# Last two token groups of an MLP as block products of Strassen's form, and state products in 64-column pieces

## The chip, the core and the metric

The kernel runs on one core of a Trainium2 chip. The metric is the device time of one execution in microseconds. The core has TensorE (PE, matrix products; weight loads are listed as PEld), VectorE (DVE), ScalarE (ACT), GpSimd (POOL) and SyncE (SP, which issues all the DMAs here). Each engine takes its instructions in the order in which they stand in its own queue.

## The reference

A gated linear recurrence over 768 tokens for 4 batches and 8 heads of 48 x 48 complex states, and then an MLP with a leaky activation on the 3072 tokens:

```python
a_re_n, a_im_n = a_re * scale, a_im * scale      # scale = min(|a|, 0.999) / (|a| + 1e-6)
for t in range(S):
    S_re, S_im = ar * S_re - ai * S_im + kv, ar * S_im + ai * S_re   # kv = k[t] outer v[t]
    y[:, :, t] = einsum('bhd,bhde->bhe', q[:, :, t], S_re)
x = y.transpose(0, 2, 1, 3).reshape(3072, 384)
h = x @ w_in                                     # 384 -> 2048
out = (max(h, 0) + alpha * min(h, 0)) @ w_out    # 2048 -> 384
```

All products are in float32. `w_in` and `w_out` come as float64 and are converted on the chip.

## The kernel before

The recurrence is cut into 24 *units* of 128 tokens (4 batches of 6). `gates` (nine stretches of tokens) makes the products of decays and phases on DVE, ACT and POOL and leaves them in DRAM; `loads` and `loads_v` bring a unit's operands back. `unit(u)` turns q and k by the phases (L663, L665), scales them in steps of doubling distance (`step`, L718), and after each pair of steps multiplies keys with queries into `ps_lv` (L680). Then it transposes the keys (`ps_kt`, L789) into the tile `T`, makes two state products per unit from `T` and `V` (`ps_kv`, L799: 64 tokens of contraction, 96 weight columns and 48 moving columns for each head and half; the last unit of a batch makes only one), applies the level products (`ps_y`, L819) and the states (`ps_y`, L843), copies the result into `T` (L857) and sends it to DRAM (`ysc`).

The MLP follows in groups of tokens: groups 0, 1 and the last two hold one unit, the ten between hold two. `loads_x` loads a group's `ysc` as `xT` (three blocks of 128 input features). `features(m, f)` makes one of the 16 blocks of 128 hidden features in three products (`ps_h`, L891), each over all tokens of the group (256 or 128 columns); ACT takes the negative part (L898) and DVE adds the leaky term into the ring `g_sb` (L900). `outputs(m, c, f)` adds one feature block to the 128 x 384 result of one unit (`ps_o`, L910); after 16 blocks ACT copies it out (L920) and SP stores it (L923).

PSUM has eight banks: `ps_lv` 2, `misc` (`ps_kt`, `ps_kv`) 1, `ps_y` 2, `ps_h` 2, `ps_o` 1. All of this is written as generators that yield once per step. `Plan.run` walks the string `ORDER`: each letter continues one generator by one step, and so the string alone sets the order in every engine's queue, the DMAs on SP included. The arguments of a yield (`PE(0.72, ...)`, `takes=`) have no effect when the kernel is built: `step` returns None. What an instruction waits for comes from the tiles that it reads and writes.

## Time and profile before

| what | value |
|---|---|
| time, median of 3 runs | 838.25 us (837.62 to 840.72) |
| profiled execution: time, span from first to last instruction | 837.42 us, 835.7 us |
| granted TensorE clock, mean | 0.992 |
| PE busy in 0:100, 300:400, 500:600, 600:700 us | 12.4, 98.2, 99.3, 100.0 us |
| DVE busy in the same stretches | 82.4, 91.2, 83.3, 61.4 us |
| `ps_h` products L891, busy | 297.4 us |
| `ps_o` products L910, busy | 295.0 us |
| `ps_kv` products L799, busy | 38.9 us |
| POOL busy after 700 us | 0 us |

The span is what the rows of the profile add up to; the time of a run also has what lies around the span. A product of float32 shows as two instructions, so 704 instructions of L799 are 352 products. "Idle before" names what ended the wait of an engine ahead of a group of instructions. A row's duration is from an instruction's start to its end; on PE consecutive ones overlap, so what one costs is read from start to start.

### The profile page before, as it was taken

How to read it: one execution, taken by the hardware profiler on the slowest of the kernel's cores; microseconds unless marked ns; L12 is line 12 of the kernel's file. 1: busy time of each engine (PE TensorE's matmuls, PEld its weight loads, DVE VectorE, ACT ScalarE, POOL GpSimd, SP SyncE). 2: the span in 40 equal slices, each digit the busy share in tenths (PEclk: the TensorE clock that was granted, in tenths of full speed). 3: DMA queues.
4: the chain of work that ended last, by engine and by line, in shares of the span. 5: the costliest groups of instructions: out<-in, count | busy, mean ns of one | idle time of the engine just before them, and what ended most of it. 6: DMA issues, size and time to landing. Idle time of an engine off the chain costs nothing.

```text
span 835.7 us, 25314 instructions
## 1 busy us (share of the span) xinstructions
PE 701.3 (84%) x10784; PEld 533.9 (64%) x10784; DVE 637.5 (76%) x905; ACT 432.4 (52%) x893; POOL 282.6 (34%) x352
## 2 busy tenths in 40 slices
PE   0001317589999999999999999999999999999998
PEld 0001316467777777777777777776777777777776
DVE  5988979999999998989978989896649555542112
ACT  7787678377556644863675366624333333323221
POOL 5379399357306620661453127303220000000000
PEclk9999999699999999999999999999999999999999
DMA  7584975885688479538863966457446635401110
GB/s 221 169 239 133 307 226 135 234 222 147 176 234 199 114 217 250 140 84 245 227 158 83 275 176 162 145 158 186 100 98 176 159 95 125 103 24 36 42 29 10
DMA packets 186984, 130.82 MB, mean 157 GB/s; under 512 B 74744, under 2 KB 177272, under 8 KB 186488
## 3 DMA queue, kind: packets, MB, share of 16 engines
q1 hardware_dynamic: 186872, 129.20, 57.6%
q8 instruction: 85, 1.39, 0.7%
q14 instruction: 27, 0.22, 0.1%
HBM read 100.82 MB, written 35.71 MB: 163 GB/s over the span
## 4 chain that ended last, share of the span: by engine, by line
PE 63%; DVE 12%; POOL 7%; DMA 7%; ACT 6%; issue 3%; SPq 2%; DVEq 0%; ACTq 0%; POOLq 0%
PE ps_o L910 25%; PE ps_h L891 24%; PE ps_lv L680 4%; POOL gate L341 3%; PE ps_kv L799 3%; PE ps_y L819 3%; DMA T<-decs 2%; DVE KQ L718 2%; PE ps_y L843 2%; POOL run L343 2%; DVE gate L341 2%; DMA PP<-phs 1%; DMA phs<-gate 1%; DVE gate L429 1%; PE ps_kt L789 1%
## 5 line engine op out<-in xcount | busy, mean ns | idle before, releaser
L891 PE MATMUL ps_h<-xT,w_in_sb 128*128 128x256 f32 (+1 forms) x1344 | 297.4, 355 | 13.7 <-DMA xT<-ysc 13.5
L910 PE MATMUL ps_o<-w_out_sb,g_sb 128*128 128x384 f32 x768 | 295.0, 499 | 3.3 <-DVE g_sb L900 2.7
L891 PEld LDWEIGHTS ps_h<-xT,w_in_sb 128*128 128x128 f32 x1344 | 234.8, 193 | 85.5 <-DMA xT<-ysc 12.9
L898 ACT ACTIVATE g_sb<-ps_h 128x256 f32<-128x256 f32 (+1 forms) x224 | 79.0, 353 | 214.4 <-PE ps_h L891 213.3
L900 DVE SCALAR_TENSOR_TENSOR g_sb<-g_sb,al,ps_h 128x256 f32<-128x256 f32 (+1 forms) x224 | 97.9, 437 | 118.9 <-ACT g_sb L898 118.3
L910 PEld LDWEIGHTS ps_o<-w_out_sb,g_sb 128*128 128x128 f32 x768 | 136.0, 191 | 56.2 <-DVE g_sb L900 4.6
L718 DVE TENSOR_TENSOR KQ<-KQ,T 96x1024 f32<-96x1024 f32 x120 | 147.8, 1232 | 27.0 <-PE ps_lv L680 16.4
L341 POOL TENSOR_TENSOR gate<-gate 128x72 f32<-128x72 f32 (+1 forms) x56 | 42.5, 759 | 177.2 <-ACT gate L371 170.9
L680 PE MATMUL ps_lv<-WQ 96*32 96x32 f32 x2304 | 34.5, 202 | 76.4 <-DVE WQ L663 53.7
L680 PEld LDWEIGHTS ps_lv<-WQ 96*32 96x32 f32 x2304 | 26.2, 115 | 98.1 <-DVE WQ L663 53.7
L741 ACT COPY WQ<-KQ 96x1024 f32<-96x1024 f32 x48 | 50.0, 1041 | 23.7 <-DVE KQ L718 23.6
L341 DVE TENSOR_TENSOR gate<-gate 128x576 f32<-128x576 f32 (+3 forms) x70 | 46.8, 669 | 1.0
L341 POOL TENSOR_TENSOR gate<-run,runs 128x12 f32<-128x12 f32 x46 | 36.8, 800 | 31.2 <-ACT runs L371 28.1
L757 ACT COPY W<-KQ 96x512 f32<-96x512 f32 x48 | 30.8, 642 | 27.3 <-DVE KQ L718 23.2
L429 DVE TENSOR_TENSOR gate<-gate 128x1152 f32<-128x1152 f32 (+2 forms) x36 | 44.5, 1257 | 0.1
L518 POOL TENSOR_SCALAR top<-top 128x768 f32<-128x768 f32 x16 | 39.7, 2486 | 14.3 <-ACT top L510 14.2
L694 ACT ACTIVATE A<-ps_lv,columns 128x64 f32<-128x64 f32 x144 | 37.6, 335 | 8.4 <-PE ps_lv L680 8.3
L799 PEld LDWEIGHTS ps_kv<-V,T 64*96 64x96 f32 x704 | 35.9, 167 | 9.1 <-issue 4.6
L857 ACT COPY T<-ps_y 48x256 f32<-48x256 f32 x96 | 32.0, 365 | 18.2 <-PE ps_y L843 17.4
L321 POOL TENSOR_TENSOR gate<-gate 128x72 f32<-128x72 f32 (+5 forms) x24 | 22.5, 939 | 54.8 <-DVE gate L321 53.8
L799 PE MATMUL ps_kv<-V,T 64*96 64x48 f32 x704 | 38.9, 252 | 2.1 <-ACT T L791 2.0
L819 PE MATMUL ps_y<-A,VL 64*48 64x64 f32 x2304 | 38.8, 221 | 0.3 <-issue 0.3
(104 smaller groups left out, 943.7 us busy)
## 6 DMA issues: line engine op xcount, KB each, us to landing
T<-decs SPq DMA_DIRECT2D x48, 384.0 KB
PP<-phs SPq DMA_DIRECT2D x24, 387.0 KB
KQ<-in_q_dram SPq DMA_DIRECT2D x48, 192.0 KB
decs<-gate SPq DMA_DIRECT2D x7, 1152.0 KB
phs<-gate SPq DMA_DIRECT2D x14, 576.0 KB
KQ<-in_k_dram SPq DMA_DIRECT2D x40, 192.0 KB
vsc<-in_v_dram SPq DMA_DIRECT2D x48, 144.0 KB
VL<-vsc SPq DMA_DIRECT2D x48, 144.0 KB
```

Source lines behind the costliest of these rows:

```text
L341: on(4 * k).tensor_tensor(out=m, in0=w[:, 1::-1].unsqueeze(2).to_broadcast([P, 2, 2, k]), in1=pairs_of(u), op=ALU.mult)
L429: TT(out=m[:, a], in0=U5[:, 1 + a], in1=turned(off3, o)[:, a].unsqueeze(1).unsqueeze(3).to_broadcast([P, L // 2, nb, 2]), op=ALU.mult)
L518: nc.gpsimd.tensor_scalar(out=top, in0=top, scalar1=F64_SMALL, scalar2=None, op0=ALU.max)
L680: nc.tensor.matmul(t[64 * i + j:64 * i + j + HC // 2, p], lhsT=keys(n, g), rhs=queries(n, g), start=True, stop=True)
L718: nc.vector.tensor_tensor(out=x, in0=x if x0 is None else x0, in1=m, op=ALU.mult)
L741: nc.scalar.copy(z.rearrange("p i n t -> p i (n t)").rearrange("p i (m h) -> p m i h", h=h), bass.AP(tensor=KQ.tensor, offset=KQ.offset + ...
L799: nc.tensor.matmul(kv[s][:, n], lhsT=T[rows, n, 0:D2], rhs=V[rows, n // 2, (n % 2) * D:(n % 2 + 1) * D], start=True, stop=True)
L819: nc.tensor.matmul(o, lhsT=Vp[h][64 * i:64 * i + 64, s, e_ * D:(e_ + 1) * D], rhs=a, start=False, stop=False)
L891: nc.tensor.matmul(p, lhsT=w_in_sb[:, f // 2, kk, f % 2 * P:(f % 2 + 1) * P], rhs=x_of[m][:, kk], start=(kk == 0), stop=(kk == NK - 1))
L898: nc.scalar.activation(gt, p, AF.Relu, scale=-1.0)
L900: nc.vector.scalar_tensor_tensor(out=gt, in0=gt, scalar=al_1[:, f:f + 1], in1=p, op0=ALU.mult, op1=ALU.add)
L910: nc.tensor.matmul(sums[0], lhsT=gt[:, c * P:(c + 1) * P], rhs=w_out_sb[:, f], start=(f == 0), stop=(f == NF - 1))
```

## The change

Groups are now 1, 1 and eleven of two units; the last two groups (units 20, 21 and 22, 23) go through `late_features` and `late_outputs`.

- `late_features(m, j)` makes two feature blocks for 256 tokens at once. The first two blocks of input features, the two units and the two feature blocks form a product of 2 x 2 by 2 x 2 blocks of 128, made with seven products (Strassen, in Winograd's form) in place of eight; the third input block is added by two products of 256 columns. They need differences of `x` (`tx`, four DVE subtractions per group) and of `w_in` (`mixes`, DVE, in a freed gate buffer). Seven partial sums lie in two PSUM banks, alternately `ps_y` and the two of `ps_h`; five DVE additions and one ACT copy join them in `g_sb`, then ACT and DVE apply the activation.
- `late_outputs` does the same for the second part: two units, two feature blocks, two halves of 192 output features. The sums of activations are made on POOL (four additions of 128 x 128 per pair of blocks, in KQ buffers), those of `w_out` in `mixes`. Seven products of 192 columns per pair add up over eight pairs in seven half banks of `ps_lv`, `misc` and `ps_o` (here `ps_m`); at the end one ACT copy and seven DVE operations make the 256 x 384 result, which goes out in two stores.
- In `unit`, a state product has its 96 weight columns extended to 128 (32 columns of the transposed keys are copied twice) and is made in two pieces of 64 columns.
- `ysc` has eight DRAM buffers in place of four, and `ORDER` is another string.

```diff
-    "AAMMBBAJAJAAMMMAJAAAAAAAAAAABAAAAAAAAAKABAKBAAAAAKABJOAKBAMAABAABAAOABLAKAOOAAKAANAABBKAABALABBABBAN"
...
+    "AABBMMAAAAAAAAAAABMMMKAAJAAABKABJAJAAKAAAAABAJBAAAANAMAKBAAKABAKANAANNBABBBABBKBBMABAKAOABLKABBALNOA"
...
+    "qqqqqqqqqqqqqqqqq")
...
-    sizes = [1, 1] + [MC] * ((NU - 4) // MC) + [1, 1]
+    sizes = [1, 1] + [MC] * ((NU - 2) // MC)
+    LATE = len(sizes) - 2
...
-            e = yield ACT(HP * D2, e, ("decays", u))
+            e = yield ACT(HP * P + 80, e, ("decays", u))
             nc.scalar.copy(T[:, 4 * i:4 * (i + 1), 0:D2], t)
+            nc.scalar.copy(T[:, 4 * i:4 * (i + 1), D2:P], t[:, :, 0:P - D2])
             R["misc"].put(e)
-        e = yield PE(0.72, e, ("V", u), *[("state", u - 1)] * (u > 0), takes=(R["misc"],) if last else (R["misc"], R["lv"]), mode=2, n=8 if last else 16)
+        e = yield PE(0.72, e, ("V", u), *[("state", u - 1)] * (u > 0), takes=(R["misc"],) if last else (R["misc"], R["lv"]), mode=2, n=16 if last else 32)
         V = L["V"]
-        kv = [ps.tile([P, H, D], F32, tag=tag, name="ps_kv", bufs=n)[0:D2] for tag, n in (("misc", 1), ("lv", 2))[:2 - last]]
+        kv = [ps.tile([P, H, D], F32, tag=tag, name="ps_kv", bufs=n) for tag, n in (("misc", 1), ("lv", 2))[:2 - last]]
         for n in range(H):
-            for s in range(1 if last else 2):
-                rows = slice(HC * s, HC * (s + 1))
-                nc.tensor.matmul(kv[s][:, n], lhsT=T[rows, n, 0:D2],
-                                 rhs=V[rows, n // 2, (n % 2) * D:(n % 2 + 1) * D], start=True, stop=True)
+            for j in range(0, P, HC):
+                for s in range(1 if last else 2):
+                    rows = slice(HC * s, HC * (s + 1))
+                    nc.tensor.matmul(kv[s][j:j + HC, n], lhsT=T[rows, n, j:j + HC],
+                                     rhs=V[rows, n // 2, (n % 2) * D:(n % 2 + 1) * D], start=True, stop=True)
...
-            nc.vector.tensor_tensor(out=St, in0=St, in1=kv[s], op=ALU.add)
+            nc.vector.tensor_tensor(out=St, in0=St, in1=kv[s][0:D2], op=ALU.add)
...
-            ysc_of[g] = dram.tile([H * D, sizes[g] * P], F32, tag="ysc", name="ysc")
+            ysc_of[g] = dram.tile([H * D, sizes[g] * P], F32, tag="ysc", name="ysc", bufs=8)
...
-        made, jobs = {}, [(m, c, f) for m, n in enumerate(sizes) for c in range(n) for f in range(NF)]
+        made, jobs = {}, [(m, c, f) for m, n in enumerate(sizes[:LATE]) for c in range(n) for f in range(NF)]
...
+    g_of = {}
+    mixed = [None]
+    HM = DM // 2
+    W2 = w_out_sb.rearrange("p (j two) (s e) -> p j two s e", two=2, s=2)
+
+    def mixes():
+
+        for j in range(0, NF // 2, 2):
+            t = yield DVE(4 * 2 * HM, ("gates", len(GATES) - 2), *[("w_out", 2 * i) for i in (j, j + 1)])
...
+            M = mixed[0][:, 0:4 * NF // 2 * HM].rearrange("p (j k e) -> p j k e", k=4, e=HM)[:, j:j + 2]
+            w = W2[:, j:j + 2]
+            for o, a, b_, op in ((M[:, :, 0], w[:, :, 0, 1], w[:, :, 0, 0], ALU.subtract),
+                                 (M[:, :, 2], w[:, :, 1, 1], w[:, :, 0, 1], ALU.subtract),
+                                 (M[:, :, 1], M[:, :, 2], w[:, :, 0, 0], ALU.add),
+                                 (M[:, :, 3], M[:, :, 1], w[:, :, 1, 0], ALU.subtract)):
+                nc.vector.tensor_tensor(out=o, in0=a, in1=b_, op=op)
...
+            t = yield DVE(4 * 2 * P, ("gates", len(GATES) - 1), *[("w_in", 2 * i) for i in (j, j + 1)])
...
+            M = mixed[1][:, 0:4 * NF // 2 * P].rearrange("p (j k e) -> p j k e", k=4, e=P)[:, j:j + 2]
+            w = w_in_sb[:, j:j + 2].rearrange("p j k (two e) -> p j k two e", two=2)
+            for o, a, b_, op in ((M[:, :, 0], w[:, :, 0, 1], w[:, :, 1, 1], ALU.add),
+                                 (M[:, :, 2], w[:, :, 0, 0], w[:, :, 0, 1], ALU.subtract),
+                                 (M[:, :, 1], M[:, :, 0], w[:, :, 0, 0], ALU.subtract),
+                                 (M[:, :, 3], w[:, :, 1, 0], M[:, :, 1], ALU.subtract)):
+                nc.vector.tensor_tensor(out=o, in0=a, in1=b_, op=op)
...
+    def late_features(m, j):
+
...
+            done["tx", m] = yield DVE(4 * P, ("x", m), takes=(R["WQ"],))
+            x = x_of[m].rearrange("p k (c t) -> p k c t", c=2)
...
+            t1, t2, t3, t4 = [tx[m][1][:, i] for i in range(4)]
+            for o, a, b_ in ((t1, x[:, 0, 1], x[:, 0, 0]), (t3, x[:, 1, 1], x[:, 0, 1]),
+                             (t2, x[:, 1, 1], t1), (t4, x[:, 1, 0], t2)):
+                TT(out=o, in0=a, in1=b_, op=ALU.subtract)
+        for at in range(9):
+            e = yield PE(0.22, ("tx", m), ("mixes", 1, j), takes=((R["h"], R["h"]) if j % 2 else (R["y"],)) if at == 0 else ())
+            if at == 0:
...
+                s1, s2, s3, s4 = [M[:, i] for i in range(4)]
+                both = x_of[m][:, 2]
+                terms = ((0, slice(0, 2), w[:, 2, 0], both), (0, 3, w[:, 0, 0], x[:, 0, 0]), (0, 0, w[:, 1, 0], x[:, 1, 0]),
+                         (0, 2, s2, t2), (0, 1, s4, x[:, 1, 1]),
+                         (1, slice(0, 2), w[:, 2, 1], both), (1, 3, s3, t3), (1, 2, s1, t1), (1, 0, w[:, 1, 1], t4))
...
+            k, place_, lhs, rhs = terms[at]
+            o = X[k][:, place_]
+            if place_ == slice(0, 2):
+                o = o.rearrange("p k t -> p (k t)")
+            nc.tensor.matmul(o, lhsT=lhs, rhs=rhs, start=(at in (0, 5)), stop=(at in (4, 8)))
...
+        r = yield ACT(P, ea, takes=(R["St"],))
...
+        nc.scalar.copy(t0, X[0][:, 3])
...
+        r = yield DVE(2 * P, r, takes=(ring, ring))
+        TT(out=pair(G, 0, 3), in0=pair(X[0], 0, 2), in1=twice(t0), op=ALU.add)
+        R["St"].put(r)
+        r = yield DVE(2 * P, e)
+        TT(out=pair(G, 1, 2), in0=pair(X[1], 2, 3), in1=twice(G[:, 3]), op=ALU.add)
+        r = yield DVE(2 * P)
+        TT(out=pair(G, 3, 2), in0=pair(X[1], 2, 0), in1=twice(G[:, 2]), op=ALU.add)
+        r = yield DVE(P)
+        TT(out=G[:, 1], in0=X[0][:, 1], in1=G[:, 1], op=ALU.add)
+        r1 = yield DVE(P)
+        TT(out=G[:, 3], in0=X[1][:, 1], in1=G[:, 3], op=ALU.add)
...
+        a1 = yield ACT(2 * P, r, takes=(R[1],))
...
+        nc.scalar.activation(rl[:, 0:2], G[:, 0:2], AF.Relu, scale=-1.0)
+        a2 = yield ACT(2 * P, r1)
+        nc.scalar.activation(rl[:, 2:4], G[:, 2:4], AF.Relu, scale=-1.0)
+        for h in range(2):
+            r = yield DVE(2 * P + 45, (a1, a2)[h])
+            g2 = G[:, 2 * h:2 * h + 2].rearrange("p f s -> p (f s)")
+            nc.vector.scalar_tensor_tensor(out=g2, in0=rl[:, 2 * h:2 * h + 2].rearrange("p f s -> p (f s)"),
+                                           scalar=al_1[:, f + h:f + h + 1], in1=g2, op0=ALU.mult, op1=ALU.add)
...
+    def late_outputs():
+
...
+        for m in range(LATE, len(sizes)):
+            for j in range(NF // 2):
+                x = yield POOL(4 * P, ("g", m, 2 * j), ("g", m, 2 * j + 1), takes=() if j % 4 else (R["KQ"],))
...
+                s1, s2, s3, s4 = [S_[:, j % 4, i] for i in range(4)]
+                for o, a, b_, op in ((s1, a21, a22, ALU.add), (s3, a11, a21, ALU.subtract),
+                                     (s2, s1, a11, ALU.subtract), (s4, a12, s2, ALU.subtract)):
+                    nc.gpsimd.tensor_tensor(out=o, in0=a, in1=b_, op=op)
+                w = W2[:, j]
+                for at in range(7):
+                    e = yield PE(0.33, x, ("mixes", 0, j), takes=() if j or at else (R["lv"], R["lv"], R["misc"], R["o"]))
...
+                        terms = ((0, 0, a11, w[:, 0, 0]), (1, 0, a12, w[:, 1, 0]), (0, 1, s2, M[:, 1]), (1, 1, s3, M[:, 2]),
+                                 (2, 0, a22, M[:, 3]), (2, 1, s1, M[:, 0]), (3, 0, s4, w[:, 1, 1]))
+                    k, half, lhs, rhs = terms[at]
+                    nc.tensor.matmul(banks[k][:, half], lhsT=lhs, rhs=rhs, start=(j == 0 and half == 0), stop=(j == NF // 2 - 1 and at in (2, 3, 5, 6)))
...
+            p1, p6, p2, p7, p4, p5, p3 = [banks[i // 2][:, i % 2] for i in range(7)]
...
+            t = yield ACT(HM, e)
+            nc.scalar.activation(tmp[:, 0], p1, AF.Copy, scale=scale)
+            for at, (o, p_, by, add) in enumerate(((ot[:, 0, 0], p2, scale, tmp[:, 0]), (tmp[:, 1], p6, scale, tmp[:, 0]),
+                                                   (tmp[:, 2], p7, scale, tmp[:, 1]), (ot[:, 1, 0], p4, -scale, tmp[:, 2]),
+                                                   (ot[:, 1, 1], p5, scale, tmp[:, 2]), (tmp[:, 3], p5, scale, tmp[:, 1]),
+                                                   (ot[:, 0, 1], p3, scale, tmp[:, 3]))):
+                t = yield DVE(HM + 60, t, takes=(R["ot"],) if at in (0, 3) else ())
+                STT(out=o, in0=p_, scalar=by, in1=add, op0=ALU.mult, op1=ALU.add)
...
         plan.add(all_mlp())
+        plan.add(mixes())
+        plan.add(late_outputs())
         plan.run(ORDER)
```

## The prediction

> **What bounds the kernel now.** First the page's total and the windows (busy us of PE, PEld, DVE, ACT, POOL, then clock, DMA share, GB/s), to see which engine limits which stage:

> ```profile
> span 835.7 us, 25314 instructions
> PE 701.3 (84%) x10784; PEld 533.9 (64%) x10784; DVE 637.5 (76%) x905; ACT 432.4 (52%) x893; POOL 282.6 (34%) x352
> ```
> ```profile
> 100.00:200.00 100.00, 60.67 (x1305) 47.86 (x1305) 92.43 (x121) 67.22 (x123) 66.84 (x68) 0.93 0.77 206
> 200.00:300.00 100.00, 98.71 (x1562) 75.73 (x1562) 94.78 (x125) 61.59 (x137) 42.78 (x52) 1.00 0.66 169
> ...
> 700.00:800.00 100.00, 100.00 (x1158) 76.00 (x1157) 36.82 (x61) 26.90 (x71) 0.00 (x0) 1.00 0.23 57
> ```
> Before 200 us PE lacks work (60.7%) while DVE is nearly full. From then on PE is full to within about 1%, at full clock: there a microsecond of PE work saved is a microsecond of time, as long as the others keep up. That PE (98.7%) and DVE (94.8%) can be full together is seen at 200:300.

> Then the chain of waits near the end (start, us, what), for what a piece costs PE when the next follows without a gap, and for the exit:

> ```profile
> 795.06 1.03 PE ps_y L843 x32
> ...
> 824.63 0.67 PE ps_h L891 x6
> 825.30 0.65 PE ps_o L910 x2
> ...
> 831.31 0.93 PE ps_o L910 x2
> 832.26 0.04 issue
> 832.31 0.49 ACT top L920
> ```
> Each float32 product is two instructions. Three 128-column feature products take 0.67 us (0.223 each), one 384-column output product 0.65 (0.645 from pieces of 1.29 for two). The last unit's `ps_y` ends at 796.1; 36.2 us of PE work follow; from PE's end the copy and the store take 3.4 us.

> TensorE's timeline (start, us, what) gives the state products (L799) and their neighbours:

> ```profile
> 601.48 0.46 PE L680 MATMUL ps_lv<-WQ 96*32 96x32 f32 x32
> 601.75 0.49 PE L680 MATMUL ps_lv<-KQ 96*32 96x32 f32 x32
> 602.17 0.91 PE L910 MATMUL ps_o<-w_out_sb,g_sb 128*128 128x384 f32 x2
> ...
> 612.79 1.56 PE L799 MATMUL ps_kv<-V,T 64*96 64x48 f32 x32
> 614.28 0.30 PE L810 MATMUL ps_y<-ident,nothing 64*48 64x256 bf16 x4
> 614.40 1.51 PE L819 MATMUL ps_y<-A,VL 64*48 64x64 f32 x96
> 615.85 1.56 PE L910 MATMUL ps_o<-w_out_sb,g_sb 128*128 128x384 f32 x4
> ```
> By start to next start, 32 `ps_kv` instructions hold PE 1.49 us (46 ns each), 96 of `ps_y` L819 only 1.45 (15 ns each): these have 48 weight columns and so run in four tiles of 64x64, the 96-column ones in two. Last, the rows by form, for the engines that get new work (busy, mean ns):

> ```profile
> L900 DVE SCALAR_TENSOR_TENSOR g_sb<-g_sb,al,ps_h 128x256 f32<-128x256 f32 x160 | 75.9, 474 | 72.2 <-ACT g_sb L898 71.8
> L831 DVE TENSOR_TENSOR St<-St,ps_kv 96x384 f32<-96x384 f32 x44 | 24.0, 545 | 5.2 <-PE ps_kv L799 4.1
> L402 POOL TENSOR_TENSOR gate<-gate 128x126 f32<-128x126 f32 x14 | 16.1, 1148 | 1.0
> L410 POOL TENSOR_TENSOR gate<-gate 128x144 f32<-128x144 f32 x7 | 5.5, 787 | 10.7 <-ACT gate L408 10.7
> ```

> **Features of the last four units.** Before, two feature blocks of 256 tokens are 6 products of 256 columns, 6 x 0.43 = 2.58 us (1.29 for three in the chain); for a single unit 6 x 0.223. After, seven of 128 and two of 256: 7 x 0.223 + 2 x 0.43 = 2.42. Group (20, 21): 8 x 0.16 = 1.3 us less. Units 22 and 23 ran alone before: 2 x 16 x 0.67 = 21.4 against 8 x 2.42 = 19.4, 2.0 less. Sum -3.3.

> **Outputs of these units.** Two blocks before: 4 x 0.645 = 2.58. After: 7 products of 192 columns; 192 has no row, and lies between 0.223 (128) and 0.43 (256); in proportion to 384, 0.323, so 2.26. 16 times 0.32: -5.2. Both parts: -8.5 us, all of it after 700 us, where PE is full. If a 192 product took as much as a 256 one, the outputs would give +6.9 instead.

> **State products.** Each unit now has 64 instructions in four tiles (32 in two for the last unit of a batch). At L819's 15 ns it is 0.97 us. Bounds: the `ps_lv` row, 64 instructions in 0.69 us; and no gain, 1.49 (64 weight columns for 48 at L819's rate would be 1.29). I take 1.0, as L819 has the same tiles: 0.49 saved per unit. PE is short of work before 200 us, when by the sum of PE's work in its order about 5 units are done; 18.5 units x 0.49 = -9.1 us (0 to -14.8). [...]
> Their cover: two more ACT copies (columns 96 to 128 of the weights) of 128x128, 0.28 us each by the form of L898 with that size; 48 x 0.28 = 13 us on ACT, 52% busy. Queued behind them on ACT are relus and WQ copies; MLP products stand between transposes and state products, so nothing on PE. Uncovered, 0.28 x 2 x 18.5 = 10 us.

> **Added work beside PE.** DVE: 32 mixes of 128x384 and 128x256, about 0.5 us, 15 us in all, where DVE has room (36.8% at 700:800). Late features per pair of blocks: three adds of 256 and two of 128 out of PSUM (0.41 and 0.28, from L831's 545 ns for 384 at 1.05 ns a column) and two multiply-adds at 0.43: 2.75 us per pair, against 2.42 of PE for features alone and 4.68 with their outputs. ACT: 0.28 + 2 x 0.38 per pair, covered. POOL: four adds of 128x128 per pair; in an undisturbed stretch (610:616) 126 columns took 0.42 us, but the means are 0.79 and 1.15: 1.8 to 4.6 us per pair; I take 2.4. DMAs on SP: the number of stores stays 24, one load of x less; no queue is passed by more.

> **The new order.** In PE's instruction order after, the last unit's `ps_y` (L848) has 52 us less PE work before it and 67.8 us behind it instead of 36.2. 25.8 us lie between it and the first features of the last group, which need its result through DRAM; before, 16.7 us (796.1 to 812.8) were enough, so that wait stays covered. Walking these 67.8 us with the prices above, the last group's outputs start 37.6 us after that `ps_y`, and the banks come free just ahead (the last by 38.2 for a use at 39.5); POOL must deliver seven further pairs between 39.8 and 66.2, 3.77 us each: covered at 2.4. DVE's work before the last unit's `ps_y`, priced by size and scaled to the page's 637.5, is 648 us against 632; between units 8 and 19 it is 277 against PE's 298 us, 93%, near to the 94.8% seen at 200:300. I allow 3 us of new stalls in all (0 to 8).

> **Exit.** The last bank is combined by a copy and seven chained adds of 192; six of them run behind the products, the rest and two stores: +1.6 (0 to 3).

> **Sum.** 835.7 - 8.5 - 9.1 + 3 + 1.6 = 822.7 us of span. The profiled run took 837.4, 1.7 more, and the median 838.25 is 0.8 above that: 822.7 + 2.5 = 825.2, say 825.

> **Rivals.**
> 1. *The gain in state products fails to arrive* (1.49 us stays, or DVE at 93% makes PE wait as much): 825 + 9 = 834. For it: DVE's share. Against: L819's row.
> 2. *GpSimd's sums become the last bound.* At 4.6 us per pair the last is ready at 39.8 + 7 x 4.6 = 72.0 for 66.2: +5.8, 831. For it: 1148 ns in the row. Against: that mean comes from stretches with DVE over 90%. [...]
> 3. *Slower: the last units do not come early enough.* The new order needs the last `ps_y` at 822.7 - 67.8 - 5 = 750, 46 us earlier than now; PE is served in order and can't go round it. Should its DVE, ACT and DMA chain move only by half, to 773, the span is 773 + 72.8 = 846 and the time 848. It is slower than before from some 13 us of delay on. For it: 277 us of DVE against 298 of PE leave little. Against: DVE was 61% busy at 600:700 and 37% after, so the slack is there.
> 4. *The split doesn't work side by side*: 64 instructions at 46 ns are 2.9 us, 18.5 x 1.45 = +27 instead of -9, 861. L819 in the same tiles speaks against it.

> **How the numbers follow.** Forecast 0.66, rival 1 0.13, rival 2 0.06, rival 3 0.12, rival 4 0.03. A measurement of this kernel tells about 0.5% (4.2 us) from no change. Faster (under 834.1): 0.66 + 0.06 + half of rival 1 less a little of the forecast's upper end = 0.76; within: 0.11; slower: 0.13. The forecast's own range is 825 - 5.7 (state products at 0.69) - 3 (no stalls) = 816, and upwards 8 us of stalls, 3 of exit: 831. To leave out no more than 2 in 10 the range takes in rival 1 and the start of rival 3: 816 to 837.

> **What would show it.** PE 20 us less busy; `ps_kv` holding about 1.0 us to the next start; seven `ps_m` products in 2.26 us and nine feature products in 2.42; the last `ps_y` at about 750; the gap from PE's last product to the end near 5 us. POOL's adds over 0.94 us each with PE waiting for them at the end would mean rival 2; PE waits for KQ, St or T in the middle, rivals 1 and 3. The forecast is wrong if PE's idle time after 200 us grows from 4 to over 15 us.

## The result and the profile after

The changed kernel took **848.21 us** (median, 847.19 to 849.23) against 838.91 us of the kernel before on the same chip: 1.011 times as long, 95% interval 1.0086 to 1.0134. The forecast said 825 and faster.

The page of the kernel after, total and engines:

```profile
span 846.3 us, 27225 instructions
PE 691.8 (82%) x11584; PEld 538.8 (64%) x11584; DVE 680.9 (80%) x1023; ACT 441.5 (52%) x939; POOL 308.7 (36%) x416
```

PE is 9.5 us less busy, and the span is 10.6 us longer. The windows (same columns as in the prediction) show where PE stands:

```profile
100.00:200.00 100.00, 58.87 (x1192) 45.94 (x1185) 88.93 (x113) 63.13 (x119) 63.32 (x73) 0.73 0.73 200
200.00:300.00 100.00, 90.88 (x1735) 70.32 (x1733) 86.98 (x120) 57.77 (x127) 42.54 (x43) 0.98 0.63 164
400.00:500.00 100.00, 94.56 (x1603) 69.72 (x1605) 86.64 (x115) 56.69 (x127) 26.99 (x38) 1.00 0.71 186
700.00:800.00 100.00, 99.43 (x1118) 79.97 (x1117) 52.73 (x114) 28.78 (x80) 14.89 (x32) 1.00 0.19 48
```

Between 200 and 300 us PE fell from 98.71 to 90.88 and VectorE from 94.78 to 86.98: nothing there got fuller, both wait more. From 200 us to the end the account is: PE busy 628.2 before, 623.3 after (-4.9); PE idle ahead of its last product 4.0 before, 18.4 after (+14.4); the exit (from PE's last product to the end) 3.4 before, 4.6 after (+1.2). That is the 10.6 us. Only 4.9 us came off after 200 us, partly because PE had done less by then: 68.5 us of work where it had done 73.1.

What PE waited for from 200 us on (total, times, longest), rows marked "issue" first in the kernel before, then after:

```profile
PE ps_y L819 <- issue: 0.3, 1, 0.3
```
```profile
PE ps_y L824 <- issue: 8.0, 5, 2.8
PE ps_lv L683 <- ACT W L760: 2.2, 2, 1.8
...
PE ps_o L915 <- issue: 1.5, 1, 1.5
...
```

So 9.5 of the 18.4 us are waits for nothing that the profile names ("issue"; what they are is shown with the experiments), and 8.9 waits for other engines and DMAs, 3.4 before.

TensorE's timeline after, one early unit and the tail:

```profile
233.31 1.15 PE L804 MATMUL ps_kv<-V,T 64*64 64x48 f32 x64
234.28 0.29 PE L815 MATMUL ps_y<-ident,nothing 64*48 64x256 bf16 x4
234.39 1.06 PE L824 MATMUL ps_y<-A,VL 64*48 64x64 f32 x61
236.89 0.76 PE L824 MATMUL ps_y<-A,VL 64*48 64x64 f32 x35 [1.43 <-issue]
...
772.51 1.10 PE L848 MATMUL ps_y<-KQ,St 96*48 96x64 f32 x32
...
837.19 0.81 PE L1090 MATMUL ps_m<-w_out_sb,g_sb 128*128 128x192 f32 x4
...
839.47 0.81 PE L1090 MATMUL ps_m<-w_out_sb,g_sb 128*128 128x192 f32 x4
...
841.42 0.49 PE L1090 MATMUL ps_m<-w_out_sb,sums 128*128 128x192 f32 x2
```

The new products cost what they should: 64 `ps_kv` instructions hold PE 0.97 us, a pair's seven `ps_m` products 839.47 - 837.19 = 2.28. But the last unit's `ps_y` (L848) comes at 772.5, not at 750, and inside the level products (L824) PE stands 1.43 us on "issue".

**VectorE in the first third.** What VectorE waited for from 60 to 300 us, first in the kernel before, then after (total, times, longest):

```profile
DVE top L520 <- POOL top L518: 5.4, 1, 5.4
DVE g_sb L900 <- ACT g_sb L898: 2.7, 6, 0.9
...
DVE gate L304 <- ACT gate L284: 1.4, 1, 1.4
...
```
```profile
DVE gate L306 <- ACT gate L286: 7.7, 2, 4.2
DVE KQ L721 <- DMA T<-decs: 4.2, 3, 1.8
DVE KQ L721 <- ACT WQ L744: 3.8, 2, 2.2
DVE KQ L721 <- PE ps_lv L683: 3.8, 5, 2.0
...
DVE WQ L666 <- DMA VL<-in_v_dram: 3.4, 1, 3.4
...
```

All rows of the two lists add up to 15.5 and 30.6 us: VectorE, which was 93% busy in that stretch before, waits 15 us more, for many things. The largest is an order fault on ScalarE, seen in ScalarE's timeline after:

```profile
74.86 0.36 ACT L410 ACTIVATE gate<-gate 128x192 f32<-128x192 f32 x1 [4.21 <-POOL gate L404]
75.13 1.15 ACT L280 ACTIVATE gate<-gate 128x1152 f32<-128x1152 f32 x1
76.31 1.25 ACT L282 ACTIVATE gate<-gate,columns 128x1152 f32<-128x1152 f32 x1
...
78.25 1.15 ACT L286 ACTIVATE gate<-gate 128x1152 f32<-128x1152 f32 x1
```

One step (L410) that waits for POOL stands ahead of the next gate stage's chain (L280 to L286), and ScalarE stands 4.2 us with work behind it that was ready.

### The profile page after: what moved, and what is told of

Same layout as the page of the kernel before. It is cut to its first block, busy times and chain, and to the rows that moved or that the text cites. A ratio compares the mean times of both kernels' runs of the same rounds, so it can differ in the third digit from the quotient of the medians.

```text
span 846.3 us, 27225 instructions
## 1 busy us (share of the span) xinstructions
PE 691.8 (82%) x11584; PEld 538.8 (64%) x11584; DVE 680.9 (80%) x1023; ACT 441.5 (52%) x939; POOL 308.7 (36%) x416
## 3 DMA queue, kind: packets, MB, share of 16 engines
q8 instruction: 91, 1.49, 0.7%
## 4 chain that ended last, share of the span: by engine, by line
PE 56%; DVE 14%; POOL 12%; DMA 7%; ACT 5%; issue 3%; SPq 2%; DVEq 0%; ACTq 0%; POOLq 0%
PE ps_o L915 18%; PE ps_h L896 17%; PE ps_m L1090 4%; POOL gate L343 4%; PE ps_lv L683 4%; PE ps_y L824 3%; POOL gate L345 3%; DVE KQ L721 2%; PE ps_kv L804 2%; PE ps_y L1015 2%; PE ps_h L1015 2%; DVE gate L343 2%; DMA PP<-phs 2%; DMA phs<-gate 2%; PE ps_y L848 2%
## 5 line engine op out<-in xcount | busy, mean ns | idle before, releaser
L896 PE MATMUL ps_h<-xT,w_in_sb 128*128 128x256 f32 (+1 forms) x1056 | 249.4, 370 | 4.1 <-DMA xT<-ysc 2.7
L915 PE MATMUL ps_o<-w_out_sb,g_sb 128*128 128x384 f32 x640 | 248.8, 504 | 4.8 <-DVE g_sb L905 3.1
L896 PEld LDWEIGHTS ps_h<-xT,w_in_sb 128*128 128x128 f32 x1056 | 191.8, 195 | 63.4 <-DMA xT<-ysc 3.2
L721 DVE TENSOR_TENSOR KQ<-KQ,T 96x1024 f32<-96x1024 f32 x120 | 148.3, 1236 | 31.9 <-PE ps_lv L683 22.1
L915 PEld LDWEIGHTS ps_o<-w_out_sb,g_sb 128*128 128x128 f32 x640 | 114.1, 191 | 49.2 <-DVE g_sb L905 4.3
L903 ACT ACTIVATE g_sb<-ps_h 128x256 f32<-128x256 f32 (+1 forms) x176 | 64.1, 364 | 134.0 <-PE ps_h L896 133.4
L905 DVE SCALAR_TENSOR_TENSOR g_sb<-g_sb,al,ps_h 128x256 f32<-128x256 f32 (+1 forms) x176 | 78.7, 448 | 37.0 <-ACT g_sb L903 36.6
L1078 POOL TENSOR_TENSOR sums<-g_sb 128x128 f32<-128x128 f32 x32 | 14.6, 477 | 197.5 <-DVE g_sb L1059 191.0
L824 PE MATMUL ps_y<-A,VL 64*48 64x64 f32 x2304 | 43.5, 222 | 11.3 <-issue 10.9
L824 PEld LDWEIGHTS ps_y<-A,VL 64*48 64x48 f32 x2304 | 39.8, 123 | 14.4 <-issue 13.2
L697 ACT ACTIVATE A<-ps_lv,columns 128x64 f32<-128x64 f32 x144 | 38.0, 336 | 12.8 <-PE ps_lv L683 12.7
L683 PE MATMUL ps_lv<-KQ,W 96*32 96x32 f32 x1536 | 24.3, 205 | 22.8 <-ACT W L760 22.7
L666 DVE TENSOR_TENSOR WQ<-KQ,PP 96x1024 f32<-96x1024 f32 x24 | 29.9, 1244 | 13.3 <-DMA VL<-in_v_dram 6.4
```

The costliest lines, as they stand in the source:

```text
L683: nc.tensor.matmul(t[64 * i + j:64 * i + j + HC // 2, p], lhsT=keys(n, g), rhs=queries(n, g), start=True, stop=True)
L697: nc.scalar.activation(a[:, :, cols], t[:, :, at:at + name], AF.Copy, scale=s)
L721: nc.vector.tensor_tensor(out=x, in0=x if x0 is None else x0, in1=m, op=ALU.mult)
L824: nc.tensor.matmul(o, lhsT=Vp[h][64 * i:64 * i + 64, s, e_ * D:(e_ + 1) * D], rhs=a, start=False, stop=False)
L896: nc.tensor.matmul(p, lhsT=w_in_sb[:, f // 2, kk, f % 2 * P:(f % 2 + 1) * P], rhs=x_of[m][:, kk], start=(kk == 0), stop=(kk == NK - 1))
L903: nc.scalar.activation(gt, p, AF.Relu, scale=-1.0)
```

## The experiments

Each ratio is against runs of the kernel before on the same chip. The spans are of one profiled run each, on several chips (medians of the kernel before there: 838.9 to 843.0 us), so the ratio decides. The columns from the profiled runs: PE busy from 200 us on; PE idle from 200 us on, without the exit of 3.4 us (old tail) or 4.6 us (new tail); VectorE busy in 60:300.

| kernel | ratio, 95% interval | span | PE busy | PE idle | DVE 60:300 |
|---|---|---|---|---|---|
| before | 1 | 835.7 | 628.2 | 4.0 | 223.7 |
| after | 1.011 [1.0086, 1.0134] | 846.3 | 623.3 | 18.4 | 208.2 |
| e1 split alone | 1.026 [1.0202, 1.0318] | 866.9 | 635.5 | 28.0 | 217.4 |
| e6 e1, shifted | 1.0242 [1.0207, 1.0277] | 861.4 | 629.7 | 28.3 | 218.6 |
| e9 e1, spread | 1.0287 [1.0259, 1.0315] | 864.3 | 650.0 | 10.9 | 217.1 |
| e4 before, new order for 7 units | 1.0182 [1.0129, 1.0234] | 854.2 | 639.6 | 11.2 | 210.7 |
| e11 the same for 4 units | 1.0114 [1.0075, 1.0154] | 852.0 | 641.3 | 7.3 | 208.8 |
| e7 the same for 2 units | 1.0055 [1.0031, 1.0079] | 840.8 | 632.9 | 4.5 | 219.0 |
| e2 after, split undone | 1.0174 [1.0123, 1.0226] | 851.0 | 634.6 | 11.7 | 209.1 |
| e5 e2, old start | 1.0032 [1.0003, 1.0061] | 839.6 | 622.9 | 12.1 | 224.7 |
| e12 e2, old order to unit 18 | 1.0207 [1.0149, 1.0265] | 851.9 | 626.4 | 20.9 | 223.0 |
| e15 e12, joined smoothly | 1.018 [1.013, 1.0229] | 852.1 | 632.1 | 15.4 | 219.9 |
| e3 after, old start | 0.9949 [0.9919, 0.998] | 836.3 | 619.4 | 12.3 | 220.3 |
| e10 e3, spread | 1.0179 [1.0153, 1.0205] | 857.5 | 640.9 | 12.0 | 214.3 |
| e14 e3, one break | 0.9955 [0.9925, 0.9985] | 831.4 | 614.8 | 12.0 | 222.6 |
| e13 after, two moves | 1.0135 [1.0095, 1.0175] | 847.6 | 620.3 | 22.7 | 210.9 |
| e8 after, extra products | 1.0232 [1.019, 1.0274] | 857.3 | 633.9 | 18.8 | 203.3 |

**Parts alone.** e1 is the kernel before with the state products of 64 columns and nothing else; e2 is the kernel after without them; e3 is the kernel after in which `ORDER` begins with the first 1529 steps of the old order (seven units) and goes on with what is left of the new; e4 is the kernel before with the first 1517 steps of the new order.

```diff
+            nc.scalar.copy(T[:, 4 * i:4 * (i + 1), D2:P], t[:, :, 0:P - D2])
...
-                nc.tensor.matmul(kv[s][:, n], lhsT=T[rows, n, 0:D2],
+            for j in range(0, P, HC):
...
+                    nc.tensor.matmul(kv[s][j:j + HC, n], lhsT=T[rows, n, j:j + HC],
```

> The kernel before with nothing but the state products split into 64-column pieces (and their second copy on ScalarE), in the order of before. Order theory (the new order's first third delays the units; the split itself pays): PE saves about 0.49 us in each of the 18 to 19 units after 200 us, 838.9 - 9 = 830 us. Split theory (the denser instruction stream starves PE of instructions, the idle marked issue inside L824, and the second copy delays the units): 838 to 850 us, with 8 us or more of PE idle marked issue.

> The changed kernel with the state products as before (96 columns, one copy), in the new order. Order theory: the saving of the split is lost, 848.2 + 9 = 857 us. Split theory: the starved stretches go, 838 to 846 us.

> The changed kernel, whose order string follows that of before until the first seven units are done and the new one from there (each step that was already taken is left out of the rest). Order theory: the lag of about 20 us that the seventh unit has in the changed kernel against its forecast falls to 5 us or less, 830 to 834 us. Split theory: nearly nothing changes, 844 to 849 us.

> The kernel before, whose order string follows the new one until the first seven units are done and its own from there. Order theory: it takes over most of the 20 us, 850 to 858 us. Split theory: 837 to 841 us, as nothing else is changed.

The order of the first seven units costs 15 us in the kernel before (e4), and giving the kernel after its old start back takes 13 us off (1.011 to 0.9949), which makes it faster than before. VectorE's waits in 60:300 go the same way: 15.5 us before and 18.4 in e3, 27.9 in e4 and 30.6 after. The split behaves in two ways. In the old order it costs 22 us (e1, beyond what either theory expected), though the state products of a unit hold PE 0.5 us less; in the new order it is worth 0.6% (e2 1.0174 against 1.011, two intervals that overlap). What it does in the old order is seen in the timeline and the group of the level products of e1:

```profile
393.90 1.17 PE L801 MATMUL ps_kv<-V,T 64*64 64x48 f32 x62
...
394.98 1.22 PE L821 MATMUL ps_y<-A,VL 64*48 64x64 f32 x68
399.90 0.65 PE L821 MATMUL ps_y<-A,VL 64*48 64x64 f32 x28 [3.70 <-issue]
```
```profile
L821 PE MATMUL ps_y<-A,VL 64*48 64x64 f32 x2304 | 43.2, 221 | 22.2 <-issue 22.1 <-DMA VL<-vsc 0.2
```

State and level products stand together there: 164 products with their weight loads, 328 instructions in about 2.5 us. PE then stands 3.7 us, and the profile shows nothing that it waits for; the only packet of its instruction queue from 389 to 401 us moved at 397 to 398, and until 397 the DMA engines were full (101.4% at 395:396). Such idle time ahead of L821 is 22.1 us in e1, 0.3 before.

What PE stands for can be counted in the traces. The 85 packets of 16 KB that this queue moved in the kernel before stand against 21780 records of TensorE (products, weight loads, 212 of its sequencer): 256 to a packet. All 17 traces together have 100 stands marked "issue". Each comes at the same record of a piece of 256, and each ends 2.2 to 3.1 us after a packet of this queue has begun to move. So PE stood there for its next piece of instructions. Full DMA engines are not needed for it: of e1's 14 stands over 0.3 us, the five longest (2.1 to 3.7) came after 4 us in which the DMA engines were full (over 100%), the nine others (0.5 to 1.8) at 1 to 67%. After 200 us, three of e1's eleven are followed by 3.4 to 6.8 us at half clock (401.2 to 404.6 here).

**Where in the order.** e5 is e3 without the split; e7 and e11 are e4 with the first two and four units.

> The changed kernel with the start of the order of before (first seven units) and the state products as before: the block products alone. If the split pays its 0.49 us per unit even with its starved stretches, this is 7 to 9 us slower than the same kernel with the split (ratio to before 1.003 to 1.006, as that one had 0.995). If the 10.6 us of PE idle marked issue and the half-clock windows behind them eat the saving, the two are equal: 0.992 to 0.998.

> The kernel before, whose order follows the new one only until the first two units are done (to about 160 us) and its own from there. If the new order loses its time there: 1.012 to 1.020 times before, as with the new order up to the seventh unit (1.018). If it loses it between the third and the seventh unit: 0.997 to 1.005.

> The kernel before with the new order for its first four units and its own for the rest. The new order for two units cost 4.6 us (1.0055), for seven units 15 (1.018). If the loss grows evenly with the units that are reordered: 7 to 10 us, ratio 1.008 to 1.012. If what is lost beyond the first two is lost in units 5 to 7 alone (from 230 us on): about 4 to 6 us, ratio 1.004 to 1.007. If it is all lost in units 3 and 4: 13 to 16 us, ratio over 1.015.

The loss grows with the units reordered: 4.6, about 10, 15 us. So it did not come in one place. VectorE's busy time in 60:300 goes with the start of the order: 203 to 211 us in every kernel with four or more units of the new start, 214 to 225 with the old one. e5 against e3 prices the split a second time: 0.8%, here clear of the intervals. e5 shows what the rest brings: PE is 5.3 us less busy after 200 us, but 8.1 us more idle, and the exit 1.2 longer.

**Late instructions.** e6 puts 64 tiny products ahead of e1, which shifts PE's instructions by 128. e9 and e10 take e1 and e3 and, from unit 5 on, put one product step of the MLP ahead of each of the four steps of level products.

> The kernel with the split alone (862 us), with 64 tiny products put in front on PE, where it waits for the first unit for over 50 us anyway: 128 instructions, so every later instruction lies 128 further in the stream of 256-instruction pieces in which PE gets its program. Page theory (PE starves where a dense stretch runs over the end of a piece while the DMA engines are full): the 26.7 us of idle marked issue change by 6 us or more, up or down, and the time with them, 840 to 875 us. Rival (any dense stretch starves, wherever it lies): 24 to 30 us of it again and 859 to 866 us.

> The split of the state products alone in the kernel before (1.026, span 866.9), with its order changed in one respect: from unit 5 on, the four steps of level products behind the state products don't follow at once, but one product step of the MLP (0.4 to 0.65 us for 6 or 2 instructions) is put ahead of each. Theory (TensorE is starved where some 300 tiny instructions stand together, 130 a microsecond): idle time put down to 'issue' ahead of the level products falls from 22.1 us to under 8, the half-clock stretches behind them go, span 832 to 845, ratio 0.995 to 1.01. Rival (the loss is in the split itself, through copies, masks or states that come late): idle time moves to other waits, span stays over 855, ratio over 1.018.

> The changed kernel with the order of before for its first seven units (0.995, span 836.3; 7.9 us of 'issue' idle ahead of the level products), and from unit 5 on one product step of the MLP ahead of each of the four steps of level products. Theory: 'issue' idle ahead of the level products falls from 7.9 to under 3 us and the half clock at 415 to 419 us goes; span 827 to 832, ratio 0.985 to 0.992. Rival (7.9 us of idle time is paid back elsewhere, since the last units' chain sets the end): span 834 to 840, ratio 0.994 to 1.003.

e6 starves at other places, as pieces of 256 would have it, and nearly as long: 22.2 us ahead of the level products and `ps_lv` for 26.7, and in the part that counts, after 200 us, 22.2 for 20.1. In e9 the theory's wait went as it said, and the time did not. Group and timeline of e9:

```profile
L821 PE MATMUL ps_y<-A,VL 64*48 64x64 f32 x2304 | 52.8, 224 | 7.9 <-issue 7.8
```
```profile
639.76 0.70 PE L893 MATMUL ps_h<-xT,w_in_sb 128*128 128x256 f32 x2
640.39 0.55 PE L821 MATMUL ps_y<-A,VL 64*48 64x64 f32 x24
640.88 0.70 PE L893 MATMUL ps_h<-xT,w_in_sb 128*128 128x256 f32 x2
641.51 0.55 PE L821 MATMUL ps_y<-A,VL 64*48 64x64 f32 x24
```

Idle fell from 22.1 to 7.8 us, but one feature product between tiles holds PE 0.63 us (639.76 to 640.39) where it holds 0.43 among its like, and 24 level products hold it 0.49 where a quarter of 96 in a row is 0.36: 0.33 us for each change from whole-array products to tiles and back. e9 has 210 such stretches of tiles for e1's 134, e10 204 for e3's 141. (A stretch of tiles is what stands between two whole-array products.) Over the whole span e9 is 21.5 us less idle and 18.9 us more busy, 0.25 us for each of 76 stretches more; e10 against e3 is 23.1 us more busy, 0.37 us for each of 63, part of which may be its lower clock before 200 us (0.74 for 0.95 in 100:200). The cure cost what the illness did.

**One break, two moves, a longer old order.** e14 breaks e3's stretch in unit 12 alone. e13 moves 7 of the 4417 steps of the kernel after: the chain L280 to L286 goes ahead of the steps on ScalarE that wait for POOL (shown above, and the same one stage later; in the diff of `ORDER` B, C and D are gate stages). e12 is e5 with the old order through unit 18, e15 the same with the MLP steps that the old order is ahead left out one by one over units 19 to 23.

```diff
-PBBBBCBBBCCOPPOPCCCNN
+PBBBCCCCBBBBOPPOPCCNN
...
-QQDQnCCLDDCQCCJOMCLOCCoLCCDDDoCL
+QQDQnDDDCCLCQCCJOMCLOCCoLCCDDoCL
```

> The changed kernel with the old order of seven units (0.995, span 836.3), where behind the state and level products of unit 12 TensorE stood 2.7 us for instructions and ran at half clock for 4 us: here three product steps of the MLP are put between the state products and the level products of that unit alone. Theory (a dense stretch is late at its place, and a break costs one switch, about 0.3 us): no issue idle at unit 12, span 831 to 834, ratio 0.989 to 0.994. Rival (the pieces of instructions then come late at another place): issue idle of the same size elsewhere, span 835 to 839, ratio 0.994 to 1.0.

> The changed kernel with 7 of its 4417 steps moved: in the order of ScalarE, the chain of one gate stage (squares and roots of 128x1152, L280 to L286) is put ahead of a step of the stage before (L410, and in the next stage L371 and L373) that waits for POOL. In the changed kernel ScalarE stood 4.2 and 4.7 us at those two steps, and VectorE then 3.5 and 4.2 us at L306 for L286. Theory (VectorE sets the time of the first third, and these two waits are half of the 15 us that it waits more than before): the wait of L306 falls from 7.7 to under 2 us, the last units come 4 to 7 us earlier, 841 to 845, ratio 1.003 to 1.007. Rival (VectorE then waits as long for the next thing, loads or copies): ratio 1.009 to 1.013 as before this edit.

> The changed kernel with one copy of the state products (96 columns, as before) and with the order of before through unit 18; the rest follows the new order. With the old order through unit 7 alone it was 1.0032 (span 839.6). Theory (the block products are worth their 8.5 us, and the new order of units 8 to 18 takes it back): span 826 to 832, ratio 0.987 to 0.995. Rival (the block products themselves, or the way the last units are placed, take it back): span 837 to 845, ratio 0.999 to 1.01.

> As the run with one copy of the state products and the old order through unit 18 (1.0207, span 851.9, of which TensorE stood 2.9 and 9.0 us at 603 to 613 us for L721 and L795, and ran at half clock behind it), but the 39 MLP steps by which the old order is ahead there are left out one by one over the units 19 to 23 instead of all at once. Theory (the block products are worth about 8.5 us, and what the new order costs is waits in units 1 to 18): TensorE's idle time from 200 us to its end 2 to 6 us, span 826 to 832, ratio 0.988 to 0.996. Rival (the block products themselves cost what they save): span over 835, ratio over 0.998, with little idle time of TensorE.

e13: the wait of L306 is gone from VectorE's list, and the others grew:

```profile
DVE KQ L721 <- ACT WQ L744: 7.9, 3, 3.3
DVE g_sb L905 <- ACT g_sb L903: 6.5, 4, 2.2
DVE KQ L721 <- PE ps_lv L683: 4.4, 4, 2.6
...
```

The rows of the list add up to 27.5 us for 30.6. Unit 7 ended 3 us earlier (301 for 304), and at 455 and 477 us PE then stood 1.8 and 3.1 us for instructions (2.8 at 478 in the kernel after); the time stayed. So taking away the largest wait did not bring the time back, as the rival said; which waits hold the start stays open. e14's break left 1.5 of 2.7 us at the same place; its profiled run is the shortest of all (831.4), its ratio that of e3 within the intervals. e12 and e15 don't tell what they were made for: where the old order joins the new, PE stands 11.8 and 6.6 us, and runs at half clock after it (mean clock in 600:700 0.90 and 0.93, in 500:600 1.00). TensorE's timeline of e12:

```profile
603.00 0.55 PE L792 MATMUL ps_kt<-ident,KQ 96*128 96x96 f32 x4 [2.85 <-DVE KQ L721]
612.52 0.90 PE L792 MATMUL ps_kt<-ident,KQ 96*128 96x96 f32 x4 [8.98 <-ACT T L794]
...
614.37 2.80 PE L802 MATMUL ps_kv<-V,T 64*96 64x48 f32 x32
...
617.30 2.78 PE L822 MATMUL ps_y<-A,VL 64*48 64x64 f32 x96
```

**Clock.** e8 adds idle products ahead of the level products of units 2 and 3, to keep PE's clock up.

> The changed kernel with 12 idle products of 128x256 in bfloat16 ahead of each level product of the second and third unit (288 more PE instructions; their results are not used), so that PE is busy in the waits between 101 and 145 us in which its granted clock is 0.50. Clock theory (half speed there costs the units 5 us or more): the clock returns to 1.00 before 115 us and the ratio falls from 1.011 to 1.000 to 1.006. Rival (the units wait for DVE and ACT there, and PE's speed is covered): 1.009 to 1.015.

The clock fell all the same (half from 124 to 141 us), and the added products took time of their own; it tells nothing of what the half clock costs. Runs of one kernel tell more: their mean clock lies near 0.97 or near 0.99, and the time does not go with it. Among the 17 runs of the kernel before beside e12 to e14, the six at 0.987 or more have a median of 842.4 us, the eleven at 0.976 or less 840.8.

**Against what was expected.** e2, e4, e5, e9 (for its time) and e11 came out as one of their sides had it, e3, e7 and e13 just beside one. e1, e6 (for its idle time), e8, e10, e12, e14 and e15 lie outside both.

## Why the forecast was wrong

The forecast span was 822.7 us, the profiled one 846.3: 23.6 us too low. Two terms make it up. PE's idle time after 200 us grew by 14.4 us where 3 were allowed (11.4 us), and PE's work after 200 us fell by 4.9 us where 17.6 were counted (12.7 us); the exit grew by 0.4 us less than forecast.

- **Prices of the new products: right.** Seven `ps_m` 2.28 us (forecast 2.26), nine feature products 2.43 (2.42), a unit's state products 0.97 (1.0), PE work behind the last `ps_y` 68.2 us (67.8), exit 4.6 (5.0). POOL's additions of 128x128 took 477 ns, 1.9 us per pair, so that rival 2 was out. The split ran side by side, so rival 4 was out too.
- **The step that failed: "I allow 3 us of new stalls in all (0 to 8)."** PE's idle time after 200 us grew by 14.4 us, to 18.4: over the 15 that the forecast named as its own end. The reason given for 3 us was a sum of VectorE's work against PE's between units 8 and 19. But most of the delay came earlier: ahead of the last `ps_y` of unit 7, PE had been idle 140.7 us (128.2 before), ahead of that of unit 24 150.2 (130.8 before), so 12.5 of 19.4 us were lost by unit 7. And of the 18.4 us after 200 us, 9.5 were late instructions, of which the forecast had no term. It compared amounts of work per stretch; what the new order changed was who waits for whom in the first third. That the order of the first units costs 13 to 15 us is shown by e3, e4, e7 and e11. That it does so through VectorE is argued, from its waits and its share of 93%; GpSimd, which has 12% of the chain that ended last for 7% before, is a rival that no run tests.
- **The second step that failed: 17.6 us of saved work counted in full.** 4.6 us of it was work that the delayed start left over for the time after 200 us (68.5 us done by then for 73.1). Over the whole span PE was 9.5 us less busy instead of 17.6. Some 3 us of that are more stretches of tiles (118 for 110 after 200 us, at 0.37 each); the rest was not separated. In 100:200 the clock was 0.73 for 0.93, so the same products hold PE longer there (in the kernel after, six `ps_h` instructions of 128 columns took 1.65 us at 134.49, at clock 0.50, and 0.83 at 149.31, at 1.00), but the runs of one kernel show no time for it.
- **"Rival 3", with 0.12, had the number**: last `ps_y` at 773 and 848 us, measured 772.5 and 848.2. That was luck: its reason (VectorE too full in the middle) did not hold. Behind unit 7 PE was idle 9.5 us, of which 6.0 were late instructions and 2.4 waits for VectorE.
- **State products, -9.1 us:** the size per unit was right, its cover wrong. "So nothing on PE" looked at ScalarE's copies and left out that twice as many instructions have to reach PE in two thirds of the time. Net the split is worth 5 us in the new order (e2 to after, not clear of noise) and 7 behind the old start (e5 to e3), and costs 22 in the old order (e1).
- **Block products, -8.5 us:** not seen as time in any run. With the old start and no split (e5) PE was 5.3 us less busy and 8.1 us more idle. Whether an order exists that keeps the gain is open; e12 and e15 failed to settle it.

Both faster versions keep all of the change's products and the old start: e3 with 0.9949 and e14 with 0.9955, each half a per cent below before.

## What to carry to other kernels

Price a new order by the stretch where another engine may set the time, and list that engine's waits, not its amount of work: here the start of the order alone cost 13 to 15 us, about what all the saved products were forecast to bring. Before cutting a product into more and smaller instructions, count how many instructions then stand together: here 328 in about 2.5 us ran ahead of TensorE's instruction queue, and putting longer products between them cost 0.25 to 0.37 us each time, as much as it brought. A part that is worth 0.6 to 0.8% in one order costs 2.6% in another, so a part and its order are to be measured together.

## What was not expected of the hardware

A long stand can be paid twice: behind 9 us of idle time in e12 the 32 state products took 2.80 us and the 96 level products 2.78, against 1.56 and 1.55 of the same forms in the kernel before (299.8 to 302.9 us).
